# The second feed-forward with its sums and low parts on VectorE instead of GpSimd

## The chip, the cores and the metric

The kernel runs on one core of a Trainium2 chip. What counts is the device time of one execution in microseconds (us), from the first to the last instruction of the slowest core; here there is one core. TensorE multiplies matrices, VectorE (DVE in rows) and GpSimd (POOL) work element by element, ScalarE (ACT) does activations and copies, SyncE (SP) issues DMAs. TensorE writes into PSUM, from which VectorE and ScalarE read.

## The reference

An input of 4 x 3072 tokens with 256 columns goes through three stages: a Fourier mix along the tokens, a gated feed-forward with token shift, and a second feed-forward, the one that changes here:

```python
def _moe2_ref(x, w_in, w_out):        # x: 12288 x 256, w_in: 256 x 2048, w_out: 2048 x 256
    h = x @ w_in
    relu6 = np.clip(h + 3.0, 0.0, 6.0)
    g = h * relu6 / 6.0
    return (g @ w_out).astype(np.float32)
```

## The kernel before

**Precision.** Each float32 operand of a product is kept as two parts in the matmul's format, a high part (a rounded copy, made by ScalarE) and a low part (the operand less its high part, a subtraction on VectorE or GpSimd). A product is then three matmuls: high by high, low by high, high by low.

**Stages.** The Fourier mix and the first feed-forward run interleaved and end at about 1060 us. Then comes the second feed-forward, tile by tile: 24 tiles of 512 tokens, each in 8 units of 256 hidden columns. A unit makes its hidden columns, gates them, splits the gated values `g` into `gh` and `gl`, and three units later these are multiplied by `w_out` (`u_o`, L724) and summed in `oacc`.

**Tile 0** uses the plain product (`u_i`, L590) into PSUM tiles `pi`. While it runs, `sums` (L613) is called once in each of the units 3 to 6, for block c = 0 to 3 of `w_in` (a block serves two units): GpSimd adds the high and low part back to full values `wa` (L624, four additions), VectorE makes four combinations `ws` (L626 to L629), ScalarE and VectorE split these into `sw` (through `split`, L147 and L148).

**Tiles 1 to 23** use a scheme after Strassen and Winograd (`u_s`, L657): 7 block products in place of 8, of blocks and block sums of the token tile (`xh`, `xl`, `th`, `tl`) and of the weights (`wi`, `sw`). With three matmuls each that is 21, to which come 24 of `u_o`, laid between them (`others`): 45 matmuls a unit. Within a unit ScalarE copies part sums from the PSUM tile `rq` to `s` three times (L686, L694, L699). The second and third product group in `rq` are written over places that ScalarE must have read: these are TensorE's only waits inside a tile. VectorE then adds `rq`, `cc` and `s` to the result `c` (L701, L702). The gate of a unit runs within the next one, as three steps handed over in `before`: ScalarE and VectorE make `g` (L713, L714), ScalarE `gh` (L718), VectorE `gl` (L719).

**Preparing the next tile.** `load_2` (L577) is called in unit 1 and brings the next token tile `xa`; `split_s` (L632) is called in unit 4. GpSimd makes four sums `xs` (L636 to L639), ScalarE copies these to `th` (L644) and the blocks to `xh` (L648), GpSimd makes the low parts `tl` (L645) and `xl` (L649).

**What sets the order.** Each engine works through its own queue in the order in which the code issues; semaphores hold an instruction until its operands are there. Nothing is reordered, so a step placed in a unit runs behind what its engine was given before it, and in front of what it is given after it. When tile 0 is done, its PSUM pool `ps` is closed and the pool `pz` for `rq` and `cc` is opened in the same place (`banks.close()`), so the first Strassen unit also waits for the last reads of tile 0's `pi`.

Of the kernel before, what the change touches and what calls it, by code (L numbers as in the profile page):

```python
# [103 lines left out]
def fourier_mix_ffn_kernel(  # L104
# [122 lines left out]
    with tc.manual_schedule(engines=order):  # L227
# [385 lines left out]
        def sums(sp, c):  # L613

            j = slice(2 * c, 2 * c + 2)
            a = sp.tile([128, 4, 2, 128], F32, tag="s", bufs=2, name="wa")
# [1 line left out]
            for k in range(2):
                for m in range(2):
                    hi, lo = (  # L620
                        w[:, k, 512 * c : 512 * c + 512].rearrange("p (j m f) -> p j m f", j=2, m=2)[:, :, m].bitcast(F32)
                        for w in (wi.hi, wi.lo)
                    )
# [1 line left out]
            a11, a12, a21, a22 = (a[:, n] for n in range(4))
            nc.vector.tensor_add(t[:, 0], a21, a22)  # L626
            nc.vector.tensor_sub(t[:, 1], t[:, 0], a11)
            nc.vector.tensor_sub(t[:, 2], a11, a21)
            nc.vector.tensor_sub(t[:, 3], a12, t[:, 1])  # L629
            split(t, sw[0][:, :, j], sw[1][:, :, j], nc.vector)  # L630

        def split_s(sp, i):  # L632

# [16 lines left out]
            blocks = {}  # L650
            for name, n in (("11", 0), ("21", 2), ("22", 3)):
                blocks[name] = (h[:, n], l[:, n])
            for name, n in (("t4", 0), ("t1", 1), ("t2", 2), ("t3", 3)):
                blocks[name] = (th[:, n], tl[:, n])
            xt[i] = blocks
# [292 lines left out]
```

## Time and profile before

| what | value |
|---|---|
| median of 3 runs | 2134.8 us (2133.62 to 2135.98) |
| the execution that was profiled, as a whole | 2136.62 us |
| its span, first to last instruction | 2134.8 us |
| busy over the span: TensorE, VectorE, ScalarE, GpSimd | 2030.0, 1555.0, 1293.8, 590.3 us |
| mean granted TensorE clock | 0.970 |

A row of a timeline gives the start, the duration, the engine, the line of the kernel, the operation, the written and the read tiles with their shapes, and in brackets how long the engine was idle before it and who released it. Matmuls overlap: a row's 0.28 us is the time from its start to its modelled end, while the next one starts some 0.12 us later. Instructions of VectorE and ScalarE also overlap by some 0.08 us at their ends.

### The profile page before, as it was taken

What the parts mean: (1) busy time and instruction counts of PE and PEld (TensorE: products, weight loads), DVE (VectorE), ACT (ScalarE), POOL (GpSimd) and SP (SyncE); (2) the same over time, 40 slices, a digit from 0 to 9 for tenths busy, and PEclk for the clock granted to TensorE, in tenths of its full rate; (3) what the DMA queues carried; (4) which work ended last, traced back from release to release, by engine and by line L of the source; (5) the groups of instructions that cost most, each with busy time, mean ns of one, the idle gap of its engine ahead of it and who ended that gap; (6) DMA issues with size and microseconds to landing.
All of it is one profiled execution on the core that took longest, in us unless ns stands there. A gap on an engine that the chain in (4) does not pass through costs nothing.

```text
span 2134.8 us, 34090 instructions
## 1 busy us (share of the span) xinstructions
PE 2030.0 (95%) x13928; PEld 1874.1 (88%) x13928; DVE 1555.0 (73%) x1681; ACT 1293.8 (61%) x1867; POOL 590.3 (28%) x453
## 2 busy tenths in 40 slices
PE   6878999999899999989979999999999999999998
PEld 4867997898788888778769999999999999999998
DVE  2988667667666687989966777777777777777775
ACT  5456457555655465555446766666666666676665
POOL 4455223222322132333341122111221122111210
PEclk7878999999999999999989999999999999999999
DMA  8765446544653352222100101001000101000100
GB/s 268 224 196 170 126 115 201 166 128 119 187 182 116 95 165 73 71 84 74 50 20 21 31 21 31 21 22 29 25 26 21 31 21 31 21 25 27 31 11 21
DMA packets 106991, 175.88 MB, mean 82 GB/s; under 512 B 12945, under 2 KB 63314, under 8 KB 106834
## 3 DMA queue, kind: packets, MB, share of 16 engines
q1 hardware_dynamic: 96034, 141.76, 21.5%
q0 software_dynamic: 10480, 31.67, 5.3%
q8 instruction: 109, 1.79, 0.4%
q14 instruction: 48, 0.39, 0.1%
q10 hardware_dynamic: 320, 0.26, 0.0%
HBM read 110.35 MB, written 63.31 MB: 81 GB/s over the span
## 4 chain that ended last, share of the span: by engine, by line
PE 63%; DVE 22%; ACT 8%; issue 4%; DMA 2%; POOL 1%; SPq 0%; ACTq 0%; DVEq 0%
PE oacc L745 17%; PE rq L745 11%; PE acc L156 9%; PE pk L156 7%; PE mix L156 4%; PE s L156 4%; PE cc L745 4%; DVE gl L719 3%; DVE g L714 3%; PE pr L156 2%; ACT g L713 2%; DVE g L549 2%; DVE xf L507 2%; DVE c L701 1%; DVE gl L550 1%
## 5 line engine op out<-in xcount | busy, mean ns | idle before, releaser
L745 PE MATMUL oacc<-wo_hi,gl 128*128 128x256 f32 x1536 | 432.9, 282 | 0.3 <-DVE gl L719 0.3
L745 PE MATMUL oacc<-wo_hi,gh 128*128 128x256 f32 x1536 | 432.1, 281 | 0.0
L745 PE MATMUL oacc<-wo_lo,gh 128*128 128x256 f32 x1536 | 430.3, 280 | 0.0
L701 DVE TENSOR_TENSOR c<-rq,s 128x512 f32<-128x512 f32 x184 | 127.3, 692 | 262.0 <-ACT s L699 262.0
L745 PEld LDWEIGHTS oacc<-wo_hi,gh 128*128 128x128 f32 x1536 | 290.3, 189 | 0.2
L745 PEld LDWEIGHTS oacc<-wo_hi,gl 128*128 128x128 f32 x1536 | 289.6, 189 | 0.7 <-DVE gl L719 0.5
L745 PEld LDWEIGHTS oacc<-wo_lo,gh 128*128 128x128 f32 x1536 | 290.0, 189 | 0.0
L718 ACT ACTIVATE gh<-g 128x1024 fp32r<-128x1024 f32 x184 | 195.1, 1060 | 155.1 <-DVE g L714 155.0
L719 DVE TENSOR_TENSOR gl<-g,gh 128x1024 fp32r<-128x1024 f32 x184 | 272.7, 1482 | 1.2 <-ACT gh L718 1.2
L745 PE MATMUL rq<-th,sw 128*128 128x256 f32 x1104 | 225.9, 286 | 27.5 <-issue 14.6
L713 ACT ACTIVATE g<-c,half 128x1024 f32<-128x1024 f32 x184 | 211.9, 1152 | 61.4 <-DVE c L702 60.4
L714 DVE SCALAR_TENSOR_TENSOR g<-g,c 128x1024 f32<-128x1024 f32 x184 | 237.0, 1288 | 15.4 <-ACT g L713 2.7
L645 POOL TENSOR_TENSOR tl<-xs,th 128x1024 fp32r<-128x1024 f32 x23 | 55.4, 2411 | 687.0 <-PE rq L745 546.7
L745 PEld LDWEIGHTS rq<-th,sw 128*128 128x128 f32 x1104 | 169.4, 189 | 36.7 <-issue 14.8
L544 ACT ACTIVATE g<-pk 128x1024 f32<-128x1024 f32 x96 | 97.9, 1019 | 151.3 <-PE pk L156 151.2
L148 POOL TENSOR_TENSOR al<-a,ah 96x512 fp32r<-96x512 f32 (+1 forms) x88 | 125.1, 1422 | 209.5 <-ACT ah L147 202.5
L156 PE MATMUL acc<-gl,wv_hi 128*128 128x512 f32 x384 | 152.8, 398 | 8.1 <-DVE gl L550 8.0
L156 PE MATMUL pk<-kh,wk_hi 128*128 128x512 f32 x384 | 152.4, 397 | 3.4 <-ACT kh L513 2.5
L745 PE MATMUL rq<-tl,sw 128*128 128x256 f32 x552 | 154.5, 280 | 0.0
L156 PE MATMUL pk<-kl,wk_hi 128*128 128x512 f32 x384 | 151.6, 395 | 1.2 <-POOL kl L514 1.2
L156 PE MATMUL acc<-gh,wv_hi 128*128 128x512 f32 x384 | 152.5, 397 | 0.0
L156 PE MATMUL acc<-gh,wv_lo 128*128 128x512 f32 x384 | 151.3, 394 | 0.0
(151 smaller groups left out, 5483.1 us busy)
## 6 DMA issues: line engine op xcount, KB each, us to landing
tt<-in_tab_dram POOLq DMA_DIRECT2D x40, 640.0 KB, 4.9
yt<-sc_y SPq DMA_DIRECT2D x23, 608.0 KB, 3.9
a<-in_x_dram SPq DMA_DIRECT2D x64, 192.0 KB, 3.3
sc_a<-s1sb SPq DMA_DIRECT2D x32, 384.0 KB, 3.7
a<-sc_a SPq DMA_DIRECT2D x48, 256.0 KB, 3.2
sc_b<-iasb SPq DMA_DIRECT2D x48, 256.0 KB, 4.9
a<-sc_b SPq DMA_DIRECT2D x64, 192.0 KB, 2.8
sc_y<-ysb SPq DMA_DIRECT2D x32, 384.0 KB, 2.8
```

What stands on the lines that cost most here:

```text
L148: eng.tensor_sub(l, src, h.bitcast(F32))
L156: nc.tensor.matmul(o, a, c, start=first and i == 0, stop=last and i == n - 1, **kw)
L507: nc.vector.scalar_tensor_tensor(o, y[:, a, 0 : hi - lo], mus[:, w, a : a + 1], o, op0=ALU.mult, op1=ALU.add)
L544: nc.scalar.activation(g, p, AF.Relu)
L549: nc.vector.tensor_mul(g, g, g)
L645: nc.gpsimd.tensor_sub(tl, t, th.bitcast(F32))
L701: nc.vector.tensor_add(c[:, 1::2], two(rq), s[:, 0:2])
L713: nc.scalar.activation(g, c, AF.Relu, bias=half, scale=1.0 / 6.0)
L714: nc.vector.scalar_tensor_tensor(g, g, 1.0, c, op0=ALU.min, op1=ALU.mult)
L718: lambda: nc.scalar.activation(h, g, AF.Copy),
L719: lambda: nc.vector.tensor_sub(l, g, h.bitcast(F32)),
L745: return lambda: nc.tensor.matmul(o, lhs, rhs, start=start, stop=stop, skip_group_check=True)
```

## The change

GpSimd gets no work of the second feed-forward any more behind tile 0's first split. `sums` and `split_s` now only lay down the tiles and return a list of steps, pairs of a function for VectorE and one for ScalarE. In tile 0 a table, `beside`, says which steps stand behind which unit: those of weight blocks 0 and 1, of the token tile 1, and the first of block 2. The other steps of block 2 and those of block 3 go into the list `aside`, of which each unit of `u_s` takes one: its VectorE part stands behind the `g` of the unit before and in front of the sums `c`, its ScalarE part behind the last copy to `s`. From tile 1 on, the three steps of the next token tile are put on that list behind unit 3. `load_2` for tile 1 is called one unit earlier. The number of matmuls, and of ScalarE's instructions, is as before.

```diff
         def sums(sp, c):
             j = slice(2 * c, 2 * c + 2)
-            a = sp.tile([128, 4, 2, 128], F32, tag="s", bufs=2, name="wa")
-            t = sp.tile([128, 4, 2, 128], F32, tag="c", bufs=2, name="ws")
...
-                    nc.gpsimd.tensor_add(a[:, 2 * m + k], hi, lo)
...
-            split(t, sw[0][:, :, j], sw[1][:, :, j], nc.vector)
+            h, l = (w[:, :, j] for w in sw)
+            tmp = {}
+
+            def full():
+                a = tmp["a"] = kb.tile([128, 4, 2, 128], F32, tag="yt", bufs=1, name="wa")
...
+                        nc.vector.tensor_add(a[:, 2 * m + k], hi, lo)
+
+            def four():
+                a11, a12, a21, a22 = (tmp["a"][:, n] for n in range(4))
+                t = tmp["t"] = sp.tile([128, 4, 2, 128], F32, tag="t", bufs=1, name="ws")
+                nc.vector.tensor_add(t[:, 0], a21, a22)
+                nc.vector.tensor_sub(t[:, 1], t[:, 0], a11)
+                nc.vector.tensor_sub(t[:, 2], a11, a21)
+                nc.vector.tensor_sub(t[:, 3], a12, t[:, 1])
+
+            return [
+                (full, None),
+                (four, lambda: nc.scalar.activation(h, tmp["t"], AF.Copy)),
+                (lambda: nc.vector.tensor_sub(l, tmp["t"], h.bitcast(F32)), None),
+            ]
 
         def split_s(sp, i):
...
-            nc.gpsimd.tensor_sub(t[:, 1], x[:, 0, 1], x[:, 0, 0])
-            nc.gpsimd.tensor_sub(t[:, 2], x[:, 1, 1], t[:, 1])
-            nc.gpsimd.tensor_sub(t[:, 3], x[:, 1, 1], x[:, 0, 1])
-            nc.gpsimd.tensor_sub(t[:, 0], x[:, 1, 0], t[:, 2])
...
-            nc.scalar.activation(th, t, AF.Copy)
-            nc.gpsimd.tensor_sub(tl, t, th.bitcast(F32))
-            flat = xt[i].rearrange("p k (t n) -> p (k t) n", t=2)
-            for n in (slice(0, 1), slice(2, 4)):
-                nc.scalar.activation(h[:, n], flat[:, n], AF.Copy)
-                nc.gpsimd.tensor_sub(l[:, n], flat[:, n], h[:, n].bitcast(F32))
...
+            def four():
+                t = tmp["t"] = sp.tile([128, 4, 256], F32, tag="t", bufs=1, name="xs")
+                nc.vector.tensor_sub(t[:, 1], x[:, 0, 1], x[:, 0, 0])
+                nc.vector.tensor_sub(t[:, 2], x[:, 1, 1], t[:, 1])
+                nc.vector.tensor_sub(t[:, 3], x[:, 1, 1], x[:, 0, 1])
+                nc.vector.tensor_sub(t[:, 0], x[:, 1, 0], t[:, 2])
+
+            def high():
+                for n in own:
+                    nc.scalar.activation(h[:, n], flat[:, n], AF.Copy)
+
+            def low():
+                for n in own:
+                    nc.vector.tensor_sub(l[:, n], flat[:, n], h[:, n].bitcast(F32))
...
+            return [
+                (four, high),
+                (low, lambda: nc.scalar.activation(th, tmp["t"], AF.Copy)),
+                (lambda: nc.vector.tensor_sub(tl, tmp["t"], th.bitcast(F32)), None),
+            ]
 
-        def u_s(sp, pz, i, j, other, before):
+        def u_s(sp, pz, i, j, other, before, aside):
...
             if before:
                 before[0]()
+            on_vector, on_scalar = aside
+            if on_vector:
+                on_vector()
             nc.scalar.activation(s[:, 0], q, AF.Copy)
...
             nc.scalar.activation(s[:, 3], q, AF.Copy)
+            if on_scalar:
+                on_scalar()
...
-                if 3 <= j < 7:
-                    sums(sp, j - 3)
+                    c0, c1, c2, c3 = (sums(sp, c) for c in range(4))
+                    x1 = split_s(sp, 1)
+                    beside = {3: c0[:2], 4: c0[2:] + c1[:1], 5: c1[1:], 6: x1[:2], 7: x1[2:] + c2[:1]}
+                    aside = c2[1:] + c3
+                if j >= 3:
+                    for on_vector, on_scalar in beside[j]:
+                        on_vector()
+                        if on_scalar:
+                            on_scalar()
...
-                before = u_s(sp, pz, i, j, u_o(*pend.pop(0)), before)
+                before = u_s(sp, pz, i, j, u_o(*pend.pop(0)), before, aside.pop(0) if aside else (None, None))
...
-                if j == 1:
+                if j == (1 if i else 0):
                     load_2(i + 1)
-                elif j == 4:
-                    split_s(sp, i + 1)
+                if j == 3 and i:
+                    aside += split_s(sp, i + 1)
```

**Where the steps stand.** VectorE in tile 4, units 4 to 6, before (g is the gate's product, c the unit's sum, gl the low part; the numbers tell tiles apart):

```order
L714 SCALAR_TENSOR_TENSOR g_12007<-g_12007,c 128x1024
L701 TENSOR_TENSOR c<-rq,s 128x2x256
L702 TENSOR_TENSOR c<-cc,s 128x2x256
L719 TENSOR_TENSOR gl_12009<-g_12007,gh_12008 128x1024
L714 SCALAR_TENSOR_TENSOR g_12068<-g_12068,c 128x1024
L701 TENSOR_TENSOR c<-rq,s 128x2x256
L702 TENSOR_TENSOR c<-cc,s 128x2x256
L719 TENSOR_TENSOR gl_12070<-g_12068,gh_12069 128x1024
L714 SCALAR_TENSOR_TENSOR g_12144<-g_12144,c 128x1024
```
and now (the lines have moved: L742 was L714, L729 and L730 were L701 and L702, L747 was L719):

```order
L742 SCALAR_TENSOR_TENSOR g_12007<-g_12007,c 128x1024
L658 TENSOR_TENSOR xs<-xa_11872 128x256
L659 TENSOR_TENSOR xs<-xa_11872,xs 128x256
L660 TENSOR_TENSOR xs<-xa_11872 128x256
L661 TENSOR_TENSOR xs<-xa_11872,xs 128x256
L729 TENSOR_TENSOR c<-rq,s 128x2x256
L730 TENSOR_TENSOR c<-cc,s 128x2x256
L747 TENSOR_TENSOR gl_12009<-g_12007,gh_12008 128x1024
L742 SCALAR_TENSOR_TENSOR g_12079<-g_12079,c 128x1024
L669 TENSOR_TENSOR xl_12011<-xa_11872,xh_12010 128x256
L669 TENSOR_TENSOR xl_12011<-xa_11872,xh_12010 128x512
L729 TENSOR_TENSOR c<-rq,s 128x2x256
```
In front of two of the sums `c` stand the four subtractions to `xs` and the two to `xl`; the one to `tl` follows in the next unit.

ScalarE at the same place, before (gh and s are its copies, o a copy of the finished output):

```order
L699 ACTIVATE s<-rq 128x256
L644 ACTIVATE th<-xs 128x1024
L648 ACTIVATE xh_12076<-xa_11872 128x256
L648 ACTIVATE xh_12076<-xa_11872 128x512
L686 ACTIVATE s<-rq 128x512
L713 ACTIVATE g_12068<-c,half 128x1024
L694 ACTIVATE s<-rq 128x256
L718 ACTIVATE gh_12069<-g_12068 128x1024
L699 ACTIVATE s<-rq 128x256
L686 ACTIVATE s<-rq 128x512
L713 ACTIVATE g_12144<-c,half 128x1024
L694 ACTIVATE s<-rq 128x256
```
and now (L709 was L686, L741 was L713, L720 was L694, L746 was L718, L725 was L699):

```order
L725 ACTIVATE s<-rq 128x256
L665 ACTIVATE xh_12010<-xa_11872 128x256
L665 ACTIVATE xh_12010<-xa_11872 128x512
L709 ACTIVATE s<-rq 128x512
L741 ACTIVATE g_12079<-c,half 128x1024
L720 ACTIVATE s<-rq 128x256
L746 ACTIVATE gh_12080<-g_12079 128x1024
L725 ACTIVATE s<-rq 128x256
L675 ACTIVATE th<-xs 128x1024
L709 ACTIVATE s<-rq 128x512
L741 ACTIVATE g_12143<-c,half 128x1024
L720 ACTIVATE s<-rq 128x256
```
The three copies that stood in a row are apart: two behind one unit's last copy to `s`, `th` a unit later.

VectorE at the end of tile 0, units 6 and 7 and the first sums of tile 1, before:

```order
L603 SCALAR_TENSOR_TENSOR g_10106<-g_10106,pi 128x1024
L148 TENSOR_TENSOR gl_10108<-g_10106,gh_10107 128x1024
L626 TENSOR_TENSOR ws<-wa 128x256
L627 TENSOR_TENSOR ws<-ws,wa 128x256
L628 TENSOR_TENSOR ws<-wa 128x256
L629 TENSOR_TENSOR ws<-wa,ws 128x256
L148 TENSOR_TENSOR sw_9953<-ws,sw_9952 128x4x256
L603 SCALAR_TENSOR_TENSOR g_10162<-g_10162,pi 128x1024
L148 TENSOR_TENSOR gl_10164<-g_10162,gh_10163 128x1024
L701 TENSOR_TENSOR c<-rq,s 128x2x256
L702 TENSOR_TENSOR c<-cc,s 128x2x256
```
and now:

```order
L603 SCALAR_TENSOR_TENSOR g_10083<-g_10083,pi 128x1024
L148 TENSOR_TENSOR gl_10085<-g_10083,gh_10084 128x1024
L658 TENSOR_TENSOR xs<-xa_9844 128x256
L659 TENSOR_TENSOR xs<-xa_9844,xs 128x256
L660 TENSOR_TENSOR xs<-xa_9844 128x256
L661 TENSOR_TENSOR xs<-xa_9844,xs 128x256
L669 TENSOR_TENSOR xl_9955<-xa_9844,xh_9954 128x256
L669 TENSOR_TENSOR xl_9955<-xa_9844,xh_9954 128x512
L603 SCALAR_TENSOR_TENSOR g_10137<-g_10137,pi 128x1024
L148 TENSOR_TENSOR gl_10139<-g_10137,gh_10138 128x1024
L676 TENSOR_TENSOR tl<-xs,th 128x1024
L629 TENSOR_TENSOR wa<-wi_hi,wi_lo 128x256 x4
```
Where block 3 of the weights was worked on, there are now the steps of token tile 1; `tl` and the first additions of block 2 stand behind the last `gl` of tile 0.

## Rows read from the trace of the kernel before

**Rows 1.** Busy time by stretch: us, then PE, PEld, DVE, ACT, POOL busy (instructions), clock, DMA

```profile
1100.00:1105.00 5.00, 2.21 (x19) 2.01 (x18) 2.70 (x4) 0.00 (x0) 5.00 (x8) 1.00 0.27 96
1105.00:1110.00 5.00, 0.00 (x0) 0.00 (x0) 3.26 (x3) 2.58 (x3) 4.44 (x5) 0.56 0.00 0
1601.00:1645.00 44.00, 43.41 (x365) 42.95 (x364) 32.29 (x33) 30.34 (x46) 9.20 (x7) 1.00 0.08 25
```
**Rows 2.** Chain of waits around the end of tile 0: start, us, what

```profile
1116.83 1.62 PE rq L745 x6
```
**Rows 3.** Timeline of VectorE in tile 0's units 3 to 7

```profile
1081.46 1.58 DVE L148 TENSOR_TENSOR gl<-g,gh 128x1024 fp32r<-128x1024 f32 x1 [1.19 <-ACT gh L147]
...
1086.83 1.21 DVE L603 SCALAR_TENSOR_TENSOR g<-g,pi 128x1024 f32<-128x1024 f32 x1
1089.23 1.23 DVE L148 TENSOR_TENSOR gl<-g,gh 128x1024 fp32r<-128x1024 f32 x1 [1.18 <-ACT gh L147]
1090.37 0.42 DVE L626 TENSOR_TENSOR ws<-wa 128x256 f32<-128x256 f32 x1
...
1091.50 0.42 DVE L629 TENSOR_TENSOR ws<-wa,ws 128x256 f32<-128x256 f32 x1
...
1102.27 0.93 DVE L626 TENSOR_TENSOR ws<-wa 128x256 f32<-128x256 f32 x1 [2.71 <-POOL wa L624]
...
1115.52 1.21 DVE L603 SCALAR_TENSOR_TENSOR g<-g,pi 128x1024 f32<-128x1024 f32 x1
```
**Rows 4.** Timeline of ScalarE there

```profile
1084.59 1.06 ACT L147 ACTIVATE sw<-ws 128x1024 fp32r<-128x1024 f32 x1 [3.16 <-DVE ws L629]
1085.56 1.10 ACT L602 ACTIVATE g<-pi,half 128x1024 f32<-128x1024 f32 x1
```
**Rows 5.** Timeline of TensorE in one tile, around `split_s`

```profile
1623.90 0.40 PE L745 MATMUL rq<-th,sw 128*128 128x256 f32 x2
...
1625.20 0.40 PE L745 MATMUL rq<-th,sw 128*128 128x256 f32 x2
...
1630.62 0.40 PE L745 MATMUL rq<-th,sw 128*128 128x256 f32 x2
...
1637.03 0.40 PE L745 MATMUL rq<-th,sw 128*128 128x256 f32 x2
...
1642.34 0.40 PE L745 MATMUL rq<-th,sw 128*128 128x256 f32 x2
```
**Rows 6.** Timeline of ScalarE in the same tile

```profile
1620.85 0.60 ACT L686 ACTIVATE s<-rq 128x512 f32<-128x512 f32 x1 [0.75 <-PE rq L745]
1621.46 1.15 ACT L713 ACTIVATE g<-c,half 128x1024 f32<-128x1024 f32 x1
1623.15 0.39 ACT L694 ACTIVATE s<-rq 128x256 f32<-128x256 f32 x1 [0.53 <-PE rq L745]
...
1626.09 0.92 ACT L648 ACTIVATE xh<-xa 128x256 fp32r<-128x256 f32 x2
...
1649.63 1.15 ACT L713 ACTIVATE g<-c,half 128x1024 f32<-128x1024 f32 x1 [0.43 <-DVE c L702]
...
1654.76 1.16 ACT L713 ACTIVATE g<-c,half 128x1024 f32<-128x1024 f32 x1 [0.25 <-DVE c L702]
```
**Rows 7.** Timeline of VectorE in the same tile

```profile
1625.27 0.69 DVE L701 TENSOR_TENSOR c<-rq,s 128x512 f32<-128x512 f32 x1 [1.40 <-ACT s L699]
...
1626.48 3.28 DVE L719 TENSOR_TENSOR gl<-g,gh 128x1024 fp32r<-128x1024 f32 x1
1629.68 1.76 DVE L714 SCALAR_TENSOR_TENSOR g<-g,c 128x1024 f32<-128x1024 f32 x1
```
**Rows 8.** Timeline of GpSimd in the same tile

```profile
1626.26 2.40 POOL L645 TENSOR_TENSOR tl<-xs,th 128x1024 fp32r<-128x1024 f32 x1 [30.27 <-ACT th L644]
```
**Rows 9.** Timeline of ScalarE, the copy to `th` in tiles 2 and 22

```profile
1189.43 1.05 ACT L644 ACTIVATE th<-xs 128x1024 fp32r<-128x1024 f32 x1
...
2060.82 1.05 ACT L644 ACTIVATE th<-xs 128x1024 fp32r<-128x1024 f32 x1
```

More of the change, by code (lines that the diff above doesn't have):

```diff
@@ L615, in sums @@
             j = slice(2 * c, 2 * c + 2)
-            a = sp.tile([128, 4, 2, 128], F32, tag="s", bufs=2, name="wa")
-            t = sp.tile([128, 4, 2, 128], F32, tag="c", bufs=2, name="ws")
[L618 to L623, printed above, removed]
-                    nc.gpsimd.tensor_add(a[:, 2 * m + k], hi, lo)
@@ L625, in sums @@
[L625 to L629, printed above, removed]
-            split(t, sw[0][:, :, j], sw[1][:, :, j], nc.vector)
+            h, l = (w[:, :, j] for w in sw)
+            tmp = {}
+            def full():
+                a = tmp["a"] = kb.tile([128, 4, 2, 128], F32, tag="yt", bufs=1, name="wa")
+                for k in range(2):
+                    for m in range(2):
+                        hi, lo = (
+                            w[:, k, 512 * c : 512 * c + 512]
+                            .rearrange("p (j m f) -> p j m f", j=2, m=2)[:, :, m]
+                            .bitcast(F32)
+                            for w in (wi.hi, wi.lo)
+                        )
+                        nc.vector.tensor_add(a[:, 2 * m + k], hi, lo)
@@ L632, in split_s @@
         def split_s(sp, i):
             x = xt[i].rearrange("p k (t n) -> p k t n", t=2)
-            t = sp.tile([128, 4, 256], F32, tag="t", bufs=1, name="xs")
-            nc.gpsimd.tensor_sub(t[:, 1], x[:, 0, 1], x[:, 0, 0])
-            nc.gpsimd.tensor_sub(t[:, 2], x[:, 1, 1], t[:, 1])
-            nc.gpsimd.tensor_sub(t[:, 3], x[:, 1, 1], x[:, 0, 1])
-            nc.gpsimd.tensor_sub(t[:, 0], x[:, 1, 0], t[:, 2])
+            flat = xt[i].rearrange("p k (t n) -> p (k t) n", t=2)
+            tmp = {}
@@ L643, in split_s @@
             tl = sp.tile([128, 4, 256], F32R, tag="tl", bufs=2, name="tl")
-            nc.scalar.activation(th, t, AF.Copy)
-            nc.gpsimd.tensor_sub(tl, t, th.bitcast(F32))
-            flat = xt[i].rearrange("p k (t n) -> p (k t) n", t=2)
-            for n in (slice(0, 1), slice(2, 4)):
-                nc.scalar.activation(h[:, n], flat[:, n], AF.Copy)
-                nc.gpsimd.tensor_sub(l[:, n], flat[:, n], h[:, n].bitcast(F32))
[L650 to L655, printed above, removed]
-        def u_s(sp, pz, i, j, other, before):
+            own = slice(0, 1), slice(2, 4)
+            def four():
[10 more added lines that the diff above has]
+                    nc.vector.tensor_sub(l[:, n], flat[:, n], h[:, n].bitcast(F32))
+            xt[i] = {n: (h[:, m], l[:, m]) for n, m in (("11", 0), ("21", 2), ("22", 3))}
+            xt[i] |= {n: (th[:, m], tl[:, m]) for m, n in enumerate(("t4", "t1", "t2", "t3"))}
+            return [
[4 more added lines that the diff above has]
+        def u_s(sp, pz, i, j, other, before, aside):
             x = xt[i]
```

## The prediction

> **What bounds the kernel now.** I read the busy time by stretch first, then the chain of waits, then the timelines of single engines in two places. In the second feed-forward TensorE is busy 43.41 of 44 us and VectorE 32.29 [rows 1]: TensorE is the bound there, and only time in which it waits can be won. There are two kinds of such time.
>
> One is a hole. In tile 0 TensorE stops 2.2 us into the stretch 1100 to 1105 and does nothing in the next one [rows 1]; it starts again at 1116.83, with the first Strassen unit [rows 2]. That is 14.6 us. It ends 0.1 us after the last read of tile 0's PSUM, the VectorE step at 1115.52 that takes 1.21 [rows 3], which stands in VectorE's queue behind the last `sums`, and these wait for GpSimd.
>
> The other comes once a tile. A unit without a wait is 5.31 us (first matmul of one unit to that of the next, 1637.03 to 1642.34). The unit behind `split_s` starts at 1625.20 and takes 5.42, the one after it 6.41 [rows 5]. The copy to `th` comes once a tile: from 1189.43 to 2060.82 are 20 tiles, 43.57 us each [rows 9], where 8 clean units would be 8 x 5.31 = 42.48. So 1.09 us a tile are lost.
>
> Why? The unit with 5.42 has ScalarE's three copies in a row (1.05 for `th`, 0.92 for the two of `xh` [rows 6, 9]). They cost TensorE 0.11. The unit with 6.41 is late by 1.10 because of VectorE: `gl` took 3.28 there and the next `g` 1.76 [rows 7], where the same shapes take 1.23 and 1.21 without GpSimd at work [rows 3]. GpSimd's `tl` ran from 1626.26 for 2.40 [rows 8], and `gl`, begun 0.2 us later, ended at 1629.76, 1.1 us after `tl`: it stood until `tl` was done. Together 2.05 + 0.53 = 2.6 us of lateness, which reach TensorE through `g`, `gh`, `s` and the copies that TensorE waits for.
>
> **The change, part by part.** *Nothing on GpSimd during the second feed-forward.* The stretching goes, whatever else happens. Where does the added VectorE and ScalarE work lie?
>
> *The steps of a tile.* Four subtractions of 128x256: four such (L626 to L629) run from 1090.37 to 1091.92 [rows 3], so 1.55 us. `low`, two subtractions of 256 and 512 columns: by the columns between 0.42 and 1.23 (256 and 1024 columns [rows 3]), about 1.1. `tl`: 1.23, as `gl` of the same size. Each stands between `g` and the sum `c` of its unit, and there VectorE sits idle 1.40 us in every unit, since `c` waits for ScalarE's `gh` and `s` [rows 7]. `low` and `tl` fit; the four overrun by 0.15. On ScalarE `high` (0.92) and `th` (1.05) come behind the last `s`, where it is idle for 0.75 before the next unit's `s` [rows 6]: overruns of 0.17 and 0.30. Added up as if none were regained, 0.62 us.
>
> How late may this get before TensorE waits? In a clean unit ScalarE finishes the gate's first pass 0.53 us before the next `s` can begin (its idle time at 1623.15); that `s` ends at 1623.54, and the matmul that needs its place starts at 1623.90 [rows 5, 6]. So 0.53 + 0.36 = 0.89, less some 0.05 for the hand-over: 0.84. That is more than 0.62. And the round ScalarE, VectorE, ScalarE, VectorE takes 5.13 when TensorE does not hold it back (1649.63 to 1654.76 [rows 6]), against 5.31: it regains 0.18 in each unit, so the tiles don't add up. I take no wait: 22 tiles prepare their successor this way (1 to 22), 22 x 1.09 = 24.0 us. The ends: 24.0, if none remains, and 0, if the same time is lost anew.
>
> *Tile 0.* I follow VectorE from the end of `gl` of unit 3, at 1081.46 + 1.23 = 1082.7 [rows 3]. A unit costs it 3.6 from the start of its `g` to the end of its `gl` (1086.83 to 1090.46 [rows 3]). A ScalarE copy that the next unit's first pass stands behind costs about 1.0 (1084.59 to 1085.56), and from that pass to `g` are 1.27 [rows 3, 4]. Additions `full` and the four of `four`: 1.5 each.
> - behind unit 3: `full`, `four` 3.0; copy to `sw`, first pass of unit 4: 2.25; `g` of unit 4 at 1087.95
> - unit 4: 3.6; low part 1.2, `full` of block 1, 1.45: 1094.2
> - unit 5: 3.6; `four` 1.5; copy 1.1; low part 1.2: 1101.6
> - unit 6: 3.6; four of the tile 1.5: 1106.7; `th` and the first pass of unit 7, with `low` beside them, 2.25: 1108.95
> - unit 7: 3.6; `tl` 1.15: 1113.7
>
> `high` waits only for the load, which is issued a unit earlier than before, and is done ahead of `four`. TensorE then needs `tl`, and starts at 1113.7 rather than 1116.8: a gain of 3.1. It comes back at the lower of its two clocks, 1.2 GHz, as before (granted clock 0.56 over the stretch in which it fell [rows 1]); the hole stays long, so I leave that price unchanged. `full` on VectorE, with its two blocks a row, isn't in the trace: 0.42 as the plain additions, or 0.93 as one beside GpSimd [rows 3]; at the high price two `full` cost 4 us more, and the gain turns into a loss of 1. If the hand-overs overlap better, 5 are won. I take 0.42, since nothing runs on GpSimd there. Blocks 2 and 3 move into tile 1 in five steps, of the same three sizes, and are needed in units 4 and 6, when they are done.
>
> **The sum.** The profiled execution's span is 2134.8, equal to the median of the runs; that execution as a whole took 2136.62, 1.8 more. Against the span: 2134.8 - 3.1 - 24.0 = 2107.7.
>
> **Rivals.**
> *The steps are not covered, and the round of VectorE and ScalarE becomes the bound.* The idle 1.40 is a wait inside that round; were it filled late, each step would lengthen it: 8 x 5.13 + 1.55 + 1.1 + 1.23 = 44.9 us a tile, 1.35 above today's 43.57. With 22 tiles and the 3.1 of tile 0: 2134.8 + 29.7 - 3.1 = 2161. It decides for slower where more than 43.57 - 41.04 = 2.5 of the 3.9 us lie bare. For it: VectorE goes from 73% of a stretch to about 82%. Against: the steps stand in the queue ahead of the wait, and begin when `g` ends.
> The Trainium skill (Perfetto Trace Analysis, section Optimizing Scalar/DVE Operations) would take work off a saturated VectorE, to ScalarE or even GpSimd, which speaks against this change; by that half of it this rival holds. It adds that GpSimd and VectorE share an SBUF read port, so that moving work between these two may not help; the `gl` of 3.28 beside `tl` agrees, and by that half the forecast holds.
>
> *Part of the wait stays.* If hand-overs double the overruns (1.24 in place of 0.62), TensorE waits 0.40 in each tile: 22 x 0.40 = 8.8, so 2116.5. It decides where the overruns pass 0.84.
>
> *The change doesn't do what it says.* The wait is as long as before, since ScalarE's copies cause it and not GpSimd: only tile 0 gains, 2131.7. Against: behind the three copies the unit was late by 0.11 alone.
>
> **How the numbers follow.** Forecast 0.76, part of the wait 0.15, no change 0.06, slower 0.03. The range runs from 2103.5 (hand-overs in tile 0 overlap, and the odd 0.1 us a tile of the clean units goes too) to 2117, the second rival's time. What a measurement here can tell from no change is 0.2%, 4.3 us: below 2130.5 is faster. The forecast and the second rival are, 0.91; the third is within, 0.06; the first slower, 0.03.
>
> **What would show it.** GpSimd empty behind the last weights of tile 0; no VectorE instruction above 1.3 us in tiles 1 to 23; units of 5.31 throughout, `th` every 42.5 us, and no TensorE wait for `s`; the first Strassen matmul near 1113.7. I am wrong if `c` no longer starts 1.40 after `g` but clearly later in the units with steps, and TensorE then waits for `s` in them; or if `full` takes 0.8 an addition, and tile 0 ends later.

## The result and the profile after

The changed kernel takes 2105.74 us, the median of four runs (2104.49 to 2106.43), against 2135.22 (2133.62 to 2135.98) beside it: a ratio of 0.9862 [0.9845, 0.9879], 29.5 us less. The forecast was 2107.7, with a range of 2103.5 to 2117. The profiled execution has a span of 2103.4 us, 31.4 below that of before.

Busy time over the span, from the page of the changed kernel:

```profile
PE 2017.2 (96%) x13928; PEld 1870.1 (89%) x13928; DVE 1579.2 (75%) x1858; ACT 1290.6 (61%) x1867; POOL 363.9 (17%) x276
```

GpSimd lost 226 us, VectorE gained 24, ScalarE lost 3. Here are stretches of the changed kernel (columns as in [rows 1]: stretch, length, busy time of TensorE, weight loads, VectorE, ScalarE and GpSimd, granted clock, DMA share, GB/s):

```profile
1100.00:1105.00 5.00, 1.33 (x12) 1.12 (x10) 3.79 (x7) 1.88 (x3) 0.00 (x0) 0.97 0.00 0
1105.00:1110.00 5.00, 0.77 (x2) 0.50 (x2) 2.63 (x5) 3.12 (x3) 0.00 (x0) 0.50 0.34 105
1110.00:1115.00 5.00, 2.90 (x13) 2.91 (x14) 4.90 (x10) 0.60 (x1) 0.00 (x0) 0.50 0.00 0
1115.00:1120.00 5.00, 5.00 (x45) 5.00 (x44) 1.29 (x2) 2.25 (x5) 0.00 (x0) 1.00 0.00 0
1601.00:1645.00 44.00, 44.00 (x376) 44.00 (x375) 33.57 (x41) 30.39 (x48) 0.00 (x0) 1.00 0.09 25
```

In the steady stretch TensorE is busy 44.00 of 44 us, where [rows 1] show 43.41, and GpSimd 0.00. The copy to `th`, once a tile, shows the tile's length (first and last of 21, ScalarE):

```profile
1187.37 1.05 ACT L675 ACTIVATE th<-xs 128x1024 fp32r<-128x1024 f32 x1
```

```profile
2036.43 1.05 ACT L675 ACTIVATE th<-xs 128x1024 fp32r<-128x1024 f32 x1
```

That is 849.06 / 20 = 42.45 us a tile, against 43.57 by [rows 9]: eight units of 5.31 with nothing between. VectorE in units 4 and 6 of one tile, and in the unit behind them, shows where the steps lie:

```profile
1604.10 1.22 DVE L742 SCALAR_TENSOR_TENSOR g<-g,c 128x1024 f32<-128x1024 f32 x1
...
1606.72 0.69 DVE L729 TENSOR_TENSOR c<-rq,s 128x512 f32<-128x512 f32 x1
...
1614.72 1.23 DVE L742 SCALAR_TENSOR_TENSOR g<-g,c 128x1024 f32<-128x1024 f32 x1 [0.27 <-ACT g L741]
1615.86 1.22 DVE L676 TENSOR_TENSOR tl<-xs,th 128x1024 fp32r<-128x1024 f32 x1
1617.34 0.69 DVE L729 TENSOR_TENSOR c<-rq,s 128x512 f32<-128x512 f32 x1 [0.26 <-ACT s L725]
...
1620.02 1.22 DVE L742 SCALAR_TENSOR_TENSOR g<-g,c 128x1024 f32<-128x1024 f32 x1 [0.26 <-ACT g L741]
1622.64 0.69 DVE L729 TENSOR_TENSOR c<-rq,s 128x512 f32<-128x512 f32 x1 [1.40 <-ACT s L725]
```

The row to look at is each `c`. Without a step it starts 2.62 us behind its `g` (1620.02 to 1622.64), after 1.40 of idleness, as in [rows 7]. With the four additions it starts 2.62 behind as well (1604.10 to 1606.72), and with `tl` too (1614.72 to 1617.34, 0.26 idle): the steps filled the gap and lengthened nothing. On ScalarE the copies behind the last `s` had room as well:

```profile
1606.59 0.93 ACT L665 ACTIVATE xh<-xa 128x256 fp32r<-128x256 f32 x2
1607.74 0.60 ACT L709 ACTIVATE s<-rq 128x512 f32<-128x512 f32 x1 [0.22 <-PE rq L773]
...
1611.90 1.05 ACT L675 ACTIVATE th<-xs 128x1024 fp32r<-128x1024 f32 x1
1613.05 0.60 ACT L709 ACTIVATE s<-rq 128x512 f32<-128x512 f32 x1
...
1618.35 0.60 ACT L709 ACTIVATE s<-rq 128x512 f32<-128x512 f32 x1 [1.05 <-PE rq L773]
```

Before a unit's first `s` (L709) ScalarE idles 1.05 us when it has no copy to make (the row at 1618.35), 0.22 behind the copies to `xh`, and the copy to `th` fits exactly.

### The profile page after: what moved, and what is told of

It is laid out like the page before. It is cut to its first block, busy times and chain, and to the rows that moved or that the text cites. A ratio compares the mean times of both kernels' runs of the same rounds, so it can differ in the third digit from the quotient of the medians.

```text
span 2103.4 us, 34043 instructions
## 1 busy us (share of the span) xinstructions
PE 2017.2 (96%) x13928; PEld 1870.1 (89%) x13928; DVE 1579.2 (75%) x1858; ACT 1290.6 (61%) x1867; POOL 363.9 (17%) x276
## 4 chain that ended last, share of the span: by engine, by line
PE 79%; DVE 12%; ACT 3%; issue 2%; DMA 2%; POOL 1%; SPq 0%; ACTq 0%; DVEq 0%
PE oacc L773 25%; PE rq L773 15%; PE acc L156 9%; PE pk L156 7%; PE cc L773 6%; PE mix L156 5%; PE s L156 4%; PE pr L156 2%; DVE g L549 2%; DVE xf L507 2%; DVE gl L550 1%; PE ia L156 1%; PE ib L419 1%; PE ib L418 1%; DVE kl L515 1%
## 5 line engine op out<-in xcount | busy, mean ns | idle before, releaser
L729 DVE TENSOR_TENSOR c<-rq,s 128x512 f32<-128x512 f32 x184 | 127.2, 691 | 184.8 <-ACT s L725 184.8
L742 DVE SCALAR_TENSOR_TENSOR g<-g,c 128x1024 f32<-128x1024 f32 x184 | 225.4, 1225 | 42.7 <-ACT g L741 37.9
L773 PE MATMUL rq<-th,sw 128*128 128x256 f32 x1104 | 221.0, 282 | 7.3 <-issue 7.3
L747 DVE TENSOR_TENSOR gl<-g,gh 128x1024 fp32r<-128x1024 f32 x184 | 223.6, 1215 | 1.2 <-ACT gh L746 1.2
L746 ACT ACTIVATE gh<-g 128x1024 fp32r<-128x1024 f32 x184 | 195.3, 1061 | 45.0 <-DVE g L742 45.0
L741 ACT ACTIVATE g<-c,half 128x1024 f32<-128x1024 f32 x184 | 210.7, 1145 | 2.2 <-DVE c L730 1.4
L709 ACT ACTIVATE s<-rq 128x512 f32<-128x512 f32 x184 | 110.2, 599 | 131.2 <-PE rq L773 129.0
```

What stands on the lines that cost most here:

```text
L709: nc.scalar.activation(s[:, 1:3].rearrange("p a n -> p (a n)"), rq, AF.Copy)
L729: nc.vector.tensor_add(c[:, 1::2], two(rq), s[:, 0:2])
L741: nc.scalar.activation(g, c, AF.Relu, bias=half, scale=1.0 / 6.0)
L742: nc.vector.scalar_tensor_tensor(g, g, 1.0, c, op0=ALU.min, op1=ALU.mult)
L746: lambda: nc.scalar.activation(h, g, AF.Copy),
L747: lambda: nc.vector.tensor_sub(l, g, h.bitcast(F32)),
```

## Experiments

All times are medians, `th` is the mean distance of 20 tiles between two copies to `th`, and the two means are those of the stretch from 1200 to 2000 us.

| kernel | us | `th`, us | `gl`, `g`, ns |
|---|---|---|---|
| before | 2135 to 2137 | 43.57 | 1491, 1289 |
| changed | 2105.7 | 42.45 | 1215, 1225 |
| e1 tile 0 alone | 2136.5 | 43.66 | 1490, 1299 |
| e2 single steps, on GpSimd | 2143.6 | 44.31 | 1596, 1290 |
| e3 on VectorE, in two units | 2115.4 | 42.76 | 1216, 1226 |
| e4 GpSimd reads beside it | 2105.9 | 42.45 | 1231, 1264 |
| e6 `tl` twice | 2104.7 | 42.45 | 1215, 1226 |
| e7 `tl` thrice | 2128.0 | 43.46 | 1215, 1225 |
| e9 single steps, GpSimd, small pieces | 2122.3 | 43.19 | 1341, 1418 |
| e10 before, GpSimd in small pieces | 2113.0 | 42.56 | 1266, 1310 |
| v1 other order in tile 0 | 2094.3 | 42.45 | 1215, 1225 |

### Which part of the change: tile 0 alone (e1)

```diff
-                if j == 3 and i:
-                    aside += split_s(sp, i + 1)
+                if j == 4 and i:
+                    split_pool(sp, i + 1)
```

`split_pool` is `split_s` as it was before.

> Tile 0 and tile 1's weights as in the changed kernel, the split of the inputs of tiles 2 to 23 on GpSimd in one go, as before. My account of the gain by place: about 5 us came from tile 0 (the hole of the matmuls before the first product of tile 1 was 14.6 us and is 10.8) and 24.6 us from the 22 steady tiles (th's copy comes round every 42.45 us instead of 43.57). So this kernel should take 2105.7 + 24.6 = 2130.3 us, between 2129 and 2132, with th's copy coming round every 43.5 us. Rival, that the steady gain came from what tile 0 does (its order carried on into the tiles): near 2106 us and a period of 42.45 us.

It measured 2136.5, a ratio of 1.0006 [0.9996, 1.0016]; I had expected 2130.3. The tiles are as long as before (43.66), so the steady gain does come from the tiles' own steps. But the gain of tile 0 doesn't show in the time. My edit itself costs something in tile 1. The sums `xs` take the memory that `ws` had (both have the tag `t`, of one buffer), so GpSimd begins them at 1138.85 only, when the last weights are split. ScalarE waits for them, once, and TensorE behind it (ScalarE's row, TensorE's first product into `cc` in that unit and in the next one, and a stretch of this kernel):

```profile
1142.79 1.06 ACT L691 ACTIVATE th<-xs 128x1024 fp32r<-128x1024 f32 x1 [4.01 <-POOL xs L686]
```

```profile
1139.38 0.28 PE L794 MATMUL cc<-xh,wi_hi 128*128 128x256 f32 x1
...
1150.23 0.28 PE L794 MATMUL cc<-xh,wi_hi 128*128 128x256 f32 x1
```

```profile
1125.00:1170.00 45.00, 40.98 (x337) 40.77 (x336) 31.00 (x39) 28.86 (x44) 12.14 (x11) 0.96 0.09 24
```

The unit takes 10.85 us, where the late unit of a tile took 6.41 before [rows 5]: 4.4 more. Some 4.0 of its time are the wait, and the clock fell in it, to a mean of 0.96 in that stretch. With the 4.4 taken off, and 0.09 a tile over the 21 tiles behind it (1.9 us; why is open), the rest is 2130.2, which accounts for the miss. Tile 0's gain is in the trace as well: TensorE's hole runs from 1100.17 to 1110.93, 10.8 us as in the changed kernel. So e1 settles the steady part by its time, and tile 0 by its trace.

### Engine or lumping: e2 and e3

In e2 the steps are issued where the change put them, but GpSimd makes them:

```diff
+            eng = nc.vector if i == 1 else nc.gpsimd
...
-                nc.vector.tensor_sub(t[:, 1], x[:, 0, 1], x[:, 0, 0])
+                eng.tensor_sub(t[:, 1], x[:, 0, 1], x[:, 0, 0])
...
-                (lambda: nc.vector.tensor_sub(tl, tmp["t"], th.bitcast(F32)), None),
+                (lambda: eng.tensor_sub(tl, tmp["t"], th.bitcast(F32)), None),
```

In e3 VectorE makes them, but lumped: three copies of ScalarE in one unit, both low parts in the next.

```diff
+            def copies():
+                nc.scalar.activation(th, tmp["t"], AF.Copy)
+                high()
+            def lows():
+                nc.vector.tensor_sub(tl, tmp["t"], th.bitcast(F32))
+                low()
+            if i > 1:
+                return [(four, copies), (lows, None)]
```

> The changed kernel's single steps, in the same units, but for tiles 2 to 23 the sums, low parts and tl on GpSimd instead of VectorE; ScalarE's copies are spread over the units as in the change. Theory A, that VectorE's own instructions stretched while GpSimd ran beside it: gl's mean stays near 1.45 us, and the matmuls wait again, 0.2 to 1.1 us per tile: 2110 to 2130 us, likeliest 2122. Theory B, that it was ScalarE's three copies in a row in one unit, which held up s and the relu square, and GpSimd cost nothing: no wait of the matmuls, 2105 to 2108 us.

> All on VectorE as in the change, but for tiles 2 to 23 the three copies of ScalarE (th and both high parts) stand in one unit and all low parts (tl and both low) in the next one on VectorE, so nothing runs on GpSimd and the work is lumped. If the lumping of the copies was the wait of before (theory B), most of it is back: 0.5 to 1.1 us per tile of waiting matmuls, 2117 to 2130 us. If only GpSimd beside VectorE was (theory A), 2105 to 2108 us. By the tolerance that I tallied (0.84 us in a unit before the matmuls wait), 1.05 + 0.93 us of copies beside each other overrun it by about 0.5 to 1.1 us, so I put 2118 us.

e2 took 2143.6, a ratio of 1.0042 [1.0025, 1.0058]: slower than the kernel before, and beyond both theories' numbers. The order of the steps is that of the change; the engine alone makes 44.31 - 42.45 = 1.86 us a tile. GpSimd's and VectorE's rows of one tile show it:

```profile
1625.67 1.99 POOL L670 TENSOR_TENSOR xl<-xa,xh 128x256 fp32r<-128x256 f32 x2 [30.56 <-ACT xh L666]
1632.26 2.41 POOL L677 TENSOR_TENSOR tl<-xs,th 128x1024 fp32r<-128x1024 f32 x1 [4.60 <-ACT th L676]
```

```profile
1626.52 2.22 DVE L748 TENSOR_TENSOR gl<-g,gh 128x1024 fp32r<-128x1024 f32 x1
...
1632.48 3.27 DVE L748 TENSOR_TENSOR gl<-g,gh 128x1024 fp32r<-128x1024 f32 x1
1635.67 1.76 DVE L743 SCALAR_TENSOR_TENSOR g<-g,c 128x1024 f32<-128x1024 f32 x1
```

`gl` beside `xl` took 2.22, `gl` beside `tl` 3.27, and the next `g` 1.76, where all three are 1.2 when GpSimd is still. (That `g` ran beside the sums `xs` of the next token tile, which GpSimd begins as soon as `tl` is made, since nothing else stands in its queue.) Before, `tl` and `xl` ran back to back and hit one unit, with 2.6 us; spread over two units they hit two `gl`, with 1.0 + 2.05 + 0.53 = 3.6 us in sum. That is 1.0 more, and the tile is 44.31 - 43.57 = 0.74 longer than before: it fits that spreading the steps, without the change of engine, made it worse for this reason, but the two `gl` were not tried apart.

e3 took 2115.4, a ratio of 0.9902 [0.9886, 0.9919], where 2118 had been expected. Its tiles are 0.31 us longer than those of the changed kernel, 6.8 of the 9.7 us. The other 3 don't come from the lumped steps: in the profiled run tile 0 ended 5.6 us later than in the changed kernel's (TensorE's hole begins at 1106.92 instead of 1101.33), ahead of all that e3 changes. `gl` and `g` are as in the changed kernel. So lumped steps, ScalarE's and VectorE's together, do cost something, about a quarter of the 1.12 us that a tile of before lost, and GpSimd beside VectorE is the larger part.

### What it is beside GpSimd that stretches: e4 and e8

e4 gives GpSimd four subtractions a tile that nobody needs; e8 gives it, by the tile's number, five forms of such work, each behind `tl`.

```diff
...
+                if j == 4 and i:
+                    junk = sp.tile([128, 256], F32, tag="junk", bufs=1, name="junk")
+                    th0, tl0 = whole[i]
+                    for m in range(4):
+                        nc.gpsimd.tensor_sub(junk, th0[:, m].bitcast(F32), tl0[:, m].bitcast(F32))
```

In e8 the target is `xs`, which is free between `tl` and the next `four`:

```diff
...
+                    r, a, b = free.bitcast(F32R), th.bitcast(F32), tl.bitcast(F32)
+                    form = i % 5
+                    if form == 0:
+                        nc.gpsimd.tensor_sub(r, a, b)
+                    elif form == 1:
+                        nc.gpsimd.tensor_sub(free, a, b)
+                    elif form == 4:
+                        nc.gpsimd.memset(free, 0.0)
+                    else:
+                        for m in range(4):
+                            nc.gpsimd.tensor_sub((r if form == 2 else free)[:, m], a[:, m], b[:, m])
```

> The changed kernel and, in unit 4 of each of tiles 1 to 23, four subtractions of 128x256 on GpSimd that nobody waits for: they read th and tl and write a scratch tile. Theory A (VectorE's instructions stretch beside GpSimd): gl or g in the unit that they fall into take longer by the time that the subtractions run, up to 2 us in all, and where that is over the slack of a unit the matmuls wait 0.3 to 1 us per tile: 2106 to 2128 us, likeliest 2112, with a longer gl in that unit in any case. Theory B: every row of VectorE as in the changed kernel, 2105 to 2107 us.

> The changed kernel and, once in each of tiles 1 to 23, work on GpSimd that nobody needs, right behind tl, in five forms by the tile's number: 0, one subtraction of 128x1024 with fp32r output (tl's own form); 1, the same with f32 output; 2, four of 128x256 with fp32r output; 3, four of 128x256 with f32 output, which in the run before stretched gl and g by 0.44 us in all over 4.9 us; 4, a memset of 128x1024. The split of before stretched gl from 1.2 to 3.28 us beside one tl of 2.40 us on GpSimd. If the type fp32r is the cause, forms 0 and 2 stretch gl and g by 1 to 2 us and forms 1, 3 and 4 by under 0.5; if the size of one instruction is, forms 0 and 1 do. The memset, which reads nothing, should leave gl and g alone. Where the stretch is over 1.31 us the matmuls wait the rest: some 0.5 to 1.2 us in up to 10 of the 23 tiles, 2106 to 2118 us.

e4 took 2105.9, a ratio of 0.9859 [0.9844, 0.9874], no different from the changed kernel, and 2112 had been thought likeliest. 4.9 us of GpSimd beside VectorE stretched `gl` and `g` by 0.44 us in all, where the split of before had stretched them by 2.6. So "VectorE is slow while GpSimd works" was too coarse, and e8 (2105.0, 0.9858 [0.9838, 0.9878]) says what matters. (2106 to 2118 had been expected; the stretch stayed under the slack in every form, and no matmul waited.) For form 0 and form 3 stand below GpSimd's row, or two of its four, then the `gl` and the `g` that ran beside it:

```profile
1702.31 2.42 POOL L961 TENSOR_TENSOR xs<-th,tl 128x1024 fp32r<-128x1024 f32 x1 [41.52 <-DVE tl L678]
```

```profile
1703.61 2.20 DVE L749 TENSOR_TENSOR gl<-g,gh 128x1024 fp32r<-128x1024 f32 x1
1705.73 1.21 DVE L744 SCALAR_TENSOR_TENSOR g<-g,c 128x1024 f32<-128x1024 f32 x1
```

```profile
1617.40 0.74 POOL L968 TENSOR_TENSOR xs<-th,tl 128x256 f32<-128x256 f32 x1 [37.64 <-DVE tl L678]
...
1618.80 1.72 POOL L968 TENSOR_TENSOR xs<-th,tl 128x256 f32<-128x256 f32 x1
```

```profile
1618.70 1.22 DVE L749 TENSOR_TENSOR gl<-g,gh 128x1024 fp32r<-128x1024 f32 x1
1620.18 1.42 DVE L744 SCALAR_TENSOR_TENSOR g<-g,c 128x1024 f32<-128x1024 f32 x1 [0.26 <-ACT g L743]
```

One subtraction of 128x1024 made `gl` 2.20 us long, whether it wrote fp32r (shown) or f32 (2.20 as well). Four of 128x256 left `gl` at 1.22 and `g` at 1.42, with either type. The memset, 0.96 us from 1659.84 on, was over before `gl` began at 1661.16, so this run doesn't test it. Between these forms the size of one GpSimd instruction decides, and not the type.

The times fit turns taken instruction by instruction: GpSimd's subtraction ends at 1702.31 + 2.42 = 1704.73, and `gl`, begun at 1703.61, ends at 1705.81, 1.08 later; alone it takes 1.21. In the kernel before, `gl` ended 1.1 us after `tl` as well [rows 7, 8]. In the other direction, of the four small subtractions the first two take 0.74 us each, and the last two, beside `gl` and `g`, 1.72: the third, begun at 1618.80, ends at 1620.52, 0.60 after `gl`. It is GpSimd that waits then. The first two ran beside the two sums `c`, which read one operand from PSUM; neither side was longer for it: `c` took 0.69 and 0.68 us, as ever, and the same beside the large subtraction of form 0. The Trainium skill (SBUF — State Buffer, section SBUF: two separate sides) states this rule: an instruction of VectorE with two inputs in SBUF and one of GpSimd that reads SBUF exclude each other, and whichever starts first holds the shared ports for the whole instruction. The rows here agree, with those 1.08, 1.1 and 0.60 us.

### A prediction from that: small pieces (e9, e10)

e9 is e2 and e10 the kernel before, both with `tl` in four pieces and `xl` in three (here e10):

```diff
-            nc.gpsimd.tensor_sub(tl, t, th.bitcast(F32))
+            for n in range(4):
+                nc.gpsimd.tensor_sub(tl[:, n], t[:, n], th[:, n].bitcast(F32))
...
             for n in (slice(0, 1), slice(2, 4)):
                 nc.scalar.activation(h[:, n], flat[:, n], AF.Copy)
+            for n in (0, 2, 3):
                 nc.gpsimd.tensor_sub(l[:, n], flat[:, n], h[:, n].bitcast(F32))
```

> The kernel with the single steps on GpSimd (2143.6 us), but each GpSimd instruction of tiles 2 to 23 is no larger than 128x256: tl in four, the low parts in three. Theory C, from the forms: an instruction of VectorE and one of GpSimd take turns, whichever began first ends first, so what counts is the length of one GpSimd instruction, not their sum. Four pieces beside gl and g cost those 0.2 to 0.44 us in all, one of 128x1024 cost gl 0.98 and in the kernel before 2.06 us. Then each unit's excess stays under the slack of 1.31 us and the matmuls never wait: 2105 to 2109 us, gl under 1.5 us on the mean. If the sum of GpSimd's time counts: 2135 to 2150 us, with gl at 1.6 us.

> The kernel before, all on GpSimd in one go and ScalarE's three copies in a row, but tl in four pieces of 128x256 and the low parts in three. Theory C: the 24.6 us of the steady tiles come back but for what the lumped copies cost (0.31 us per tile in the run with two units, 6.8 us), tile 0's hole stays as it was: 2135 - 24.6 + 6.8 = 2117 us, between 2109 and 2122. If the sum of GpSimd's time counts: 2132 to 2140 us.

e10 took 2113.0, a ratio of 0.9887 [0.9871, 0.9904], within what theory C gave: 22 of the 29.5 us that the change won come from cutting `tl` and `xl`, with all of the work still on GpSimd and ScalarE's three copies still in a row. In the tile below `gl` is 1.60 long in one unit and `g` 1.59 in the next (1.58 in the one behind), where they were 3.28 and 1.76 in one and the same unit (VectorE, e10):

```profile
1614.00 1.60 DVE L721 TENSOR_TENSOR gl<-g,gh 128x1024 fp32r<-128x1024 f32 x1
...
1621.22 1.59 DVE L716 SCALAR_TENSOR_TENSOR g<-g,c 128x1024 f32<-128x1024 f32 x1
```

e9 took 2122.3, 0.9938 [0.9922, 0.9953]: the cut won 21 us against e2, but 2105 to 2109 had been expected. The step that failed is "each unit's excess stays under the slack": `gl` and `g` of three units in a row are stretched (VectorE, e9):

```profile
1615.94 1.66 DVE L752 TENSOR_TENSOR gl<-g,gh 128x1024 fp32r<-128x1024 f32 x1
1617.53 1.76 DVE L747 SCALAR_TENSOR_TENSOR g<-g,c 128x1024 f32<-128x1024 f32 x1
...
1621.89 1.60 DVE L752 TENSOR_TENSOR gl<-g,gh 128x1024 fp32r<-128x1024 f32 x1
1623.42 1.75 DVE L747 SCALAR_TENSOR_TENSOR g<-g,c 128x1024 f32<-128x1024 f32 x1
...
1627.77 1.42 DVE L752 TENSOR_TENSOR gl<-g,gh 128x1024 fp32r<-128x1024 f32 x1
1629.12 1.75 DVE L747 SCALAR_TENSOR_TENSOR g<-g,c 128x1024 f32<-128x1024 f32 x1
```

Against 1.22 and 1.23 these are 0.44 + 0.53, 0.38 + 0.52 and 0.20 + 0.52, together 2.6 us. The first pair ran beside `xl`, the second beside `tl`, the third beside the sums `xs` of the next token tile. No single one reaches the slack, but a unit regains little (the round of VectorE and ScalarE takes 5.13 of a unit's 5.31 us [rows 6]), so the lateness adds up from unit to unit: TensorE's units behind these are 5.40, 5.57 and 5.69 us long instead of 5.31, 0.74 a tile in sum. (Why the first of them waits at all, at 0.97, is open.) Pieces let the other engine in between, but each of VectorE's instructions may then wait for one piece.

### How large the slack is: e6 and e7

```diff
+            def last():
+                for _ in range(2 if i > 1 else 1):
+                    nc.vector.tensor_sub(tl, tmp["t"], th.bitcast(F32))
```

In e7 the 2 is a 3.

> The changed kernel with tl written twice for tiles 2 to 23: one useless subtraction more (1.22 us on VectorE) in the unit of tl. It measures the slack on which the prediction rested. I tallied 0.84 us of tolerance in a unit; in the trace of the changed kernel ScalarE idles 1.05 us before the first s of a unit and VectorE 0.26 us before c in tl's unit. By the tally 1.22 - 0.84 = 0.4 us per tile waits: 2114 us. By what stands in the changed kernel's rows (0.26 + 1.05 = 1.31 us) nothing waits: 2105 to 2107 us, and I take this one.

> As the kernel with tl twice, but thrice: 2.44 us more on VectorE in tl's unit. With a slack of 0.84 us the matmuls wait 1.6 us per tile: 2141 us; with 1.31 us they wait 1.13 us: 2130 us. Either way the excess over the slack should come out in the time one for one; if VectorE were covered more deeply (a wait that a later unit gives back) it would be under 2115 us.

e6 took 2104.7 and e7 2128.0 (0.9853 [0.9839, 0.9868] and 0.9966 [0.9953, 0.9979]), both close to what the rows of the changed kernel gave. In e6 `c` came late and no TensorE wait followed in the steady tiles; in e7, VectorE's rows of `tl`'s unit, `tl` three times in one row:

```profile
1622.84 1.23 DVE L746 SCALAR_TENSOR_TENSOR g<-g,c 128x1024 f32<-128x1024 f32 x1 [0.27 <-ACT g L745]
1623.98 3.74 DVE L675 TENSOR_TENSOR tl<-xs,th 128x1024 fp32r<-128x1024 f32 x3
1627.63 0.68 DVE L733 TENSOR_TENSOR c<-rq,s 128x512 f32<-128x512 f32 x1
```

`c` starts 4.79 behind `g` instead of 2.62, so 2.17 late, and the tile is 1.01 longer: 1.16 us were absorbed. In e6 `c` was 0.92 late (3.54 behind `g`), and all of it was absorbed. So the slack is about 1.2 us, not the 0.84 that I tallied, and VectorE can take the 1.22 us of e6 more in that unit for nothing.

### The hole of tile 0: another order (v1)

The steps come singly here: of `sums` `full`, `four`, the copy and the low part, of `split_s` `four`, `high`, `low`, the copy to `th` and `tl`, counted from 0.

```diff
-                    beside = {3: c0[:2], 4: c0[2:] + c1[:1], 5: c1[1:], 6: x1[:2], 7: x1[2:] + c2[:1]}
-                    aside = c2[1:] + c3
+                    beside = {
+                        3: (c0[0], c0[1]),
+                        4: (c0[2], c0[3], x1[0], x1[1]),
+                        5: (x1[2], x1[3]),
+                        6: (x1[4],),
+                        7: (c1[0], c1[1]),
+                    }
...
```

What is left of c1, c2 and c3 stands in tile 1, units 0 to 5.

> The changed kernel with another order of the single steps at the end of tile 0: the first pair of weight sums and the split of tile 1's inputs first, one to two units earlier, the other three pairs of weights later, in tile 1's units 0 to 5. If the hole of the matmuls (from 1101.3 to 1112.1 us in the changed kernel) is only the end of VectorE's queue at tl, it goes: matmuls of tile 1 follow at once, 10.8 us less, and the full clock does not fall, some 1.5 us less; tile 1 may give back 1 to 2 us where two steps stand in one unit. 2094 to 2097 us. If the hole is set by something else (ScalarE's copies, the inputs of tile 1), 2103 to 2107 us.

2094.3 us, a ratio of 0.9810 [0.9794, 0.9827], so it beats both kernels. Stretches of v1, and TensorE's first product into `cc` in two units of its tile 1, five units apart:

```profile
1100.00:1105.00 5.00, 5.00 (x45) 5.00 (x44) 4.55 (x10) 2.04 (x5) 0.00 (x0) 1.00 0.00 0
1105.00:1110.00 5.00, 5.00 (x44) 5.00 (x44) 4.63 (x9) 3.87 (x6) 0.00 (x0) 1.00 0.02 3
```

```profile
1115.78 0.28 PE L779 MATMUL cc<-xh,wi_hi 128*128 128x256 f32 x1
...
1144.25 0.28 PE L779 MATMUL cc<-xh,wi_hi 128*128 128x256 f32 x1
```

TensorE runs at the full clock through the ten microseconds in which it nearly stood still in both other kernels. Those five units, which the steps of the weights now share, take 28.47 us where clean ones take 26.55, so tile 1 gives 1.9 back. The traces add up to 10.8 for the hole, and 0.8 for the clock (the first Strassen unit takes 5.31 instead of 6.15), less 1.9: 9.7 us, and from the last of tile 0's own products to the end they differ by 9.75. The profiled run of v1 was 2.1 us ahead before that, in stages that both kernels share, so the 11.4 us between the medians may hold some luck. Nothing in the work itself demanded the hole: the steps were in the wrong order in VectorE's queue, and `tl`, which the first Strassen unit needs at once, stood last.

## Why the prediction was right

**The steady tiles: 24.0 forecast, 24.6 measured.** The mechanism held step by step: no stretched `gl`, units of 5.31, `th` every 42.45 us (42.48 forecast), (43.57 - 42.45) x 22 = 24.6. e2 shows that the engine caused the wait, e10 that it was two long instructions of it, and e3 and e10 that ScalarE's copies in a row cost 0.1 to 0.3 a tile at most; the forecast had read 0.11 for them from [rows 5].

**The tally of lateness was mis-sized, on the safe side, twice.** The overruns were put at 0.62 us: 0.15 for the four additions, 0.17 and 0.30 for the copies. The rows show none: `c` comes 2.62 behind `g` either way, and ScalarE's idle time before a unit's first `s` is 1.05 and not 0.75 once TensorE sets the pace. I had read the 0.75 of [rows 6] in a unit in which ScalarE was still catching up: in that tile of before its idle time there grows by 0.17 a unit (0.22 at 1604.93, 0.39 at 1610.24, 0.75 at 1620.85), and the next tile's GpSimd work cuts it off before it gets to 1.05. And the slack was put at 0.84 where e7 shows 1.16. The trace of before had said so: 2.6 us of lateness cost 1.10 there, so some 1.5 were absorbed there (why 0.3 more than in e7 is open). Two smaller readings were off as well. The sign "if `c` no longer starts 1.40 after `g`" takes VectorE's idle time for a distance: `c` starts 2.62 after `g`, of which 1.40 are idle. And VectorE was to rise to about 82% of a stretch; it is 76% (33.57 of 44), since 2.6 us of stretched time a tile went as 3.9 us of steps came.

**Tile 0: 3.1 forecast, about 5.4 measured.** This is the term that was too small: 2.3 of the 2.9 us by which the two terms together fell short. The steps of VectorE in tile 0 of the changed kernel:

```profile
1080.28 1.23 DVE L148 TENSOR_TENSOR gl<-g,gh 128x1024 fp32r<-128x1024 f32 x1 [1.19 <-ACT gh L147]
1081.42 1.43 DVE L629 TENSOR_TENSOR wa<-wi_hi,wi_lo 128x256 f32<-128x256 f32 x4
...
1110.82 1.22 DVE L676 TENSOR_TENSOR tl<-xs,th 128x1024 fp32r<-128x1024 f32 x1
```

From the start of `gl` of unit 3 to the end of `tl` the forecast had 1113.7 - 1081.46 = 32.2, the trace has 1112.04 - 1080.28 = 31.8: the chain was right to 0.5 us, and `full` (L629) is indeed as cheap as the plain additions, 1.43 for four. The rest of the term is what I had set to nothing (TensorE's rows at the end of the hole):

```profile
1108.60 0.77 PE L773 MATMUL rq<-th,sw 128*128 128x256 f32 x2 [7.27 <-issue]
1112.10 0.58 PE L773 MATMUL rq<-tl,sw 128*128 128x256 f32 x1 [2.73 <-DVE tl L676]
```

Two matmuls that need only `th` ran at 1108.60 already, inside the hole. And the full clock came back sooner: the granted clock is 1.00 from 1115 on, 2.9 us after the restart at 1112.10. The kernel before restarts at 1116.83 and shows 0.74 in the stretch from 1120 on, which is half the clock until about 1122.6, 5.8 us after the restart:

```profile
1115.00:1120.00 5.00, 3.17 (x15) 3.20 (x16) 2.96 (x3) 2.00 (x3) 0.00 (x0) 0.50 0.00 0
1120.00:1125.00 5.00, 5.00 (x34) 5.00 (x34) 0.50 (x1) 0.77 (x2) 0.00 (x0) 0.74 0.00 0
```

The hole itself shrank from 14.6 to 10.8, so 3.8. TensorE's first product into `cc` comes 1.02 us after the restart instead of 1.42, since the two matmuls had been made: 0.4. From there to the same product of the next unit it takes 6.15 us instead of 7.28: 1.1 for the clock. Together that is about 5.4.

The last of the three was luck. e2, e4 and e6 have the same steps in tile 0, the same hole and the same two matmuls in it, and there the full clock came back 6.0 to 6.2 us after the restart; in e1, e3, e7, e8 and e9 it came 2.8 to 3.1 us after it. Here is e6, TensorE's restart and a stretch that begins 3 us behind it:

```profile
1108.31 0.58 PE L777 MATMUL rq<-tl,sw 128*128 128x256 f32 x1 [2.73 <-DVE tl L675]
```

```profile
1111.30:1114.30 3.00, 3.00 (x16) 3.00 (x16) 0.00 (x0) 0.38 (x1) 0.00 (x0) 0.50 0.00 0
```

So about 4.2 of the 5.4 us belong to the change, and the forecast's 3.1 was short by about 1.1 of its own. What is left of the 31.4 in the spans, about 1.4, lies in stages that the change doesn't touch and at the end: the changed kernel's run was 0.9 us ahead at 1101, when TensorE stops.

**The rivals.** *Steps not covered* (2161) fell: filling the 1.40 us didn't lengthen the round, since `c` waits for a `gh` that was on its way. e7 shows where it would begin, at some 1.2 us more in one unit. *Part of the wait stays* (2116.5) fell with the overruns. *ScalarE's copies are the cause* (2131.7) fell with e2 and e10. The half of the rule of the Trainium skill (Perfetto Trace Analysis, section Optimizing Scalar/DVE Operations) that speaks against the change, to take work off a saturated VectorE, didn't apply: VectorE went from 73 to 75% of the span, and what counts is the 1.40 us in each unit in which it waited for ScalarE.

## What to carry to other kernels

An instruction that takes twice its usual time, with no wait named, is worth more than the row of waits: look which instruction of GpSimd ran beside it and how long that one is. Before work is moved from GpSimd to VectorE, try to cut it: short pieces off the critical path hold VectorE up for one piece, long ones for their whole length. And when a queue feeds an engine that stands still, first ask which of its steps that engine needs at once, and put those first: by the traces of v1 this was worth 10 us more.
